# Sign of a converted weight by a VectorE mask and a GpSimd add, routing in three portions, ones by GpSimd

## The chip, the core and the metric

One core of a Trainium2 chip runs the whole program. The metric is device microseconds for one execution, as the median of several runs.

## The reference, cut to what matters

```python
def phi(x):                                   # per head, 64 -> 128 -> 256 features
    proj = x @ w_phi
    proj = proj - max(abs(proj))
    return concat([exp(proj), exp(-proj)])
kv = phi(k).T @ v;  z = sum(phi(k))           # per batch and head
attn = (phi(q) @ kv) / (phi(q) @ z + 1e-06)   # 4 x 8 x 576 x 64
x = attn as [2304, 512]
e = argmax(x @ w_gate);  gate = softmax prob of e     # 8 experts
y = gate * (relu(x @ w1[e]) @ w2[e])          # at most `capacity` tokens per expert
h = y @ w_in;  out = (h - tanh(h)) @ w_out    # 512 -> 2048 -> 512
```

`w_in` and `w_out` arrive as 64-bit floats. The kernel reads each as two 32-bit words, makes an fp32 number of it on the chip, and splits that into a high and a low part for products in three matmuls.

## The kernel before, in words

There are two stages. In the **attention stage** (about the first 183 us) a loop over steps `s` works on 18 chunks of 128 tokens. Step `i` issues to TensorE (PE), in this order: the projection of the keys of chunk `i` into the PSUM pair `xb` (L303), the transposes of an earlier query chunk (L378), the products keys times values of chunk `i-1` (L346), the projection of the queries of chunk `i-5`, again into `xb`, the numerators (L445), and a small gate product of chunk `i` (L332). Each projection is followed on VectorE (DVE) by a reduction and a subtraction out of `xb` (L311, L314), here called "k pair" and "q pair"; the next projection into `xb` waits for the subtraction. ScalarE (ACT) does the exponentials (L322, L323 for keys, L384 for queries) and the evacuations. The third engine with data work is GpSimd (POOL), and SP issues most DMAs. All engines work in program order; the order is written by hand in the loop at L747 to L842.

Woven into steps 4 to 17 is the conversion of 13 pieces of weights of 128x1024 (`pieces`, `CV`). ACT scales the high word into `a` (L91) and takes its sign into a bf16 tile `m` (L94); DVE shifts `a` left (L98, right after the k pair) and or-s in the top bits of the low word (L100, at the end of the step); GpSimd multiplies `a` by `m` (L104). In the next step ACT copies `a` into the high part (L274) and GpSimd subtracts it from `a` for the low part (L277).

Routing (`route1`) is a chain of small DVE instructions on three chunks at once. For groups of chunks 0 to 2, 3 to 5 and 6 to 8 it runs after the q pair and before L100: five portions of the generator (6 instructions, L486 to L496) in the first step after the group's numerators are out, the other 8 in the next step.

A values tile `v` has three buffers. Its DMA (L241) also writes over a column of ones and the gate columns, and ACT fills both after it landed: the gate columns by L336, the ones by L337, at the end of step `i`. Two chunks (4 and 13) straddle two batches; each uses two of the tiles, whose other half DVE sets to zero (L240). So the tiles of chunks 5, 6, 14 and 15, and the second ones of 4 and 13, are loaded one step later than the others.

In the **expert stage** the experts and the two last weight products run over units of 576 slots; here six more rows of `w_out` are converted (`late_bits`, L1112), four with GpSimd's multiply and two with DVE's.

Of the kernel before, what the change touches and what calls it, by code (L numbers as in the profile page):

```python
# [37 lines left out]
def build(nc, tc, ctx, qT, kT, vT, v, w_phi, w_gate, w12, win, wout, out, cap):  # L38
# [46 lines left out]


    NP = 512

    def cv_size(t, a):

        nc.scalar.activation(out=a.bitcast(F32), in_=t[:, :, 1].bitcast(F32), func=AF.Copy, scale=2.0 ** -112)  # L91

    def cv_sign(t, m):
        nc.scalar.activation(out=m, in_=t[:, :, 1].bitcast(F32), func=AF.Sign)  # L94

    def cv_bits(t, a, m, eng=nc.gpsimd):

        nc.vector.tensor_scalar(out=a, in0=a, scalar1=3, scalar2=None, op0=ALU.logical_shift_left)  # L98
        yield
        nc.vector.scalar_tensor_tensor(out=a, in0=t[:, :, 0], scalar=29, in1=a,  # L100
                                       op0=ALU.logical_shift_right, op1=ALU.bitwise_or)
        yield
        af = a.bitcast(F32)
        eng.tensor_tensor(out=af, in0=af, in1=m, op=ALU.mult)  # L104
        yield

    def cv_split(af, fh, fl, eng=nc.gpsimd):
# [29 lines left out]
    def attention():  # L137
# [97 lines left out]
        def ldv(c, a):  # L235
            t = vuse[c][a]
            lo, hi = (64 * a, 64 * a + 64) if c in strad else (0, P)
            if c in strad:
                z = 64 - 64 * a
                nc.vector.memset(t[z:z + 64, :, 0:HB], 0.0)  # L240
            nc.sync.dma_start(out=t[lo:hi].rearrange("p h d -> p (h d)"), in_=v[c, lo:hi])  # L241

        def ldq(c):
# [18 lines left out]
        def cv_mag(i):  # L262
            if i in raw:
                a = cva[i] = cv.tile([P, NPC], I32, tag="a", name="a")
                m = cvm[i] = cv.tile([P, NPC], BF16, tag="m", name="m")
                cvw[i] = a.bitcast(F32)
                cv_size(raw[i], a)
                cv_sign(raw[i], m)

        def cv_main(i):  # L270
            yield from cv_bits(raw.pop(i), cva.pop(i), cvm.pop(i))
# [27 lines left out]
        def proj(kind, i, ps):  # L299
            src = (kin if kind == "k" else qin)[i]  # L300
            for hp in range(4):
                for g in range(2):
                    nc.tensor.matmul(ps[:, g, hp * DF:(hp + 1) * DF],  # L303
                                     src[64 * g:64 * g + 64, hp * P:(hp + 1) * P], wphi[64 * g:64 * g + 64],
                                     start=(hp == 0), stop=(hp == 3), skip_group_check=True)
            psk[kind, i] = ps.rearrange("p g (a b) -> p (g a) b", b=DF)
# [12 lines left out]
        def kexp(i):  # L319
# [3 lines left out]
            nc.scalar.activation(out=e[:, :, 1, :], in_=t, func=AF.Exp, scale=-1.0)  # L323
            kp[i] = e

        def vgate(c):
            vg = sb[:, 0:4 * GP].rearrange("p (a b) -> p a b", b=GP)
            ps = vg[:, :, 0:2 * E].rearrange("p a (b e) -> p a b e", e=E)
            for hp in range(4):
                for a in range(2):  # L330
                    o = hp * P + 64 * a
                    nc.tensor.matmul(vg[64 * a:64 * a + 64, hp, :], vtin[c][:, o:o + 64], wgb[:, hp],  # L332
                                     start=(hp == 0), stop=(hp == 3), skip_group_check=True)
            for a, t in enumerate(vuse[c]):
                lo, hi = (64 * a, 64 * a + 64) if c in strad else (0, P)
                nc.scalar.copy(t[lo:hi, :, D + 1:HB].rearrange("p (a b) e -> p a b e", b=2), ps[lo:hi])  # L336
                nc.scalar.copy(t[lo:hi, :, D:D + 1], ones[lo:hi, 0:H].unsqueeze(2))  # L337

        def kv(i, vt, first, last):
            for g in range(2):  # L340
# [406 lines left out]
        for s in range(LAST + 1):  # L747
            i, j, jt = s, s - LAG, s - LAG - 1
            jn = jt if s < SD else jt - 1 if s > SD else -1
            kk, qq, tt = i < NCH, 0 <= j < NCH, 0 <= jt < NCH  # L750
            pc, pd = CV.get(s), CV.get(s - 1)
            since = {cs: s - (cs[-1] + LAG + 1) for cs in subs}
            if s == SK:
                stk.close()
                mo["alloc"]()
                qpools.append(stq.enter_context(tc.tile_pool(name="qp2", bufs=1)))
                mo["spare"](qpools[-1])
                mo["rows"](zero)
            if kk:
                proj("k", i, xb if i > LAG or i % 2 == 0 else yb)  # L760
            if tt:
                trans(jt)
                qexp(jt, 0)
                qexp(jt, 1)
            if since[subs[-1]] == 3:
                prefix(early)
            if 0 <= i - 1 < NCH - 1:
                kv_step(i - 1)
            if kk:
                for _ in sub("k", i):  # L770
                    pass
            bits = iter(()) if pc is None else cv_main(pc)
            next(bits, None)
            if qq:
                proj("q", j, xb)
            if i - 1 in strad:
                kv_second(i - 1)
            if i == NCH:
                kv_step(i - 1)
                first_ids()  # L780
            if pd is not None:
                cv_hi(pd)
                cv_lo(pd)
            if kk:
                kexp(i)
            wgen = iter(())
            if since[subs[-1]] == 3:
                wgen = itertools.chain(route2(early), table(early))
                run(itertools.islice(wgen, 5))
            if qq:  # L790
                for _ in sub("q", j):
                    pass
            smalls = []
            for cs in subs:
                d = since[cs]
                if d == 1:
                    rgen[cs] = route1(early, cs[0], cs[-1] + 1)
                    smalls.append(itertools.islice(rgen[cs], 5))
                if d == 2:
                    smalls.append(rgen[cs])  # L800
            smalls.append(wgen)
            if s == NCH:
                smalls.append(fgen["t"])
            if s == SK:
                smalls.append(fgen["u"])
            weave([], smalls)
            flush()
            for _ in bits:
                pass
            if 0 <= jn < NCH:  # L810
                num(jn)
            if kk:
                vgate(i)
            if CV.get(s + 1) is not None:
                cv_mag(CV[s + 1])
            if s + 2 < NCH:
                ldk(s + 2)
            if 0 <= j + 2 < NCH:
                ldq(j + 2)
            if pc is not None:  # L820
                cv_load(pc + NRAW)
            if s == SK:
                mo["first"]()
            if s + 2 < NCH:
                ldvt(s + 2)
            for c, a in vslot.get(s, []):
                if c > 1:
                    ldv(c, a)
            if s in (2, 3):
                cv_load(s - 2)  # L830
            if 0 <= jn < NCH:
                xstore([jn])
            for c in zeros.get(s, ()):
                nc.sync.dma_start(out=out[c * P:(c + 1) * P, :].rearrange("t (a b) -> t a b", a=4),
                                  in_=zero.unsqueeze(1).to_broadcast([P, 4, P]))
            if s >= SK:
                mo["drain"](s - SK)
            if s == SK + 3:
                rgen["a"] = route1(tailg, 0, NA)
                run(itertools.islice(rgen["a"], 5))  # L840
            if s == SK + 4:
                run(rgen["a"])  # L842
# [9 lines left out]
    def experts():  # L852
# [252 lines left out]

        def late_tiles(f):
            if f in lord[LF:]:
                return rawt[0][:, 0:NP].bitcast(I32), rawt[1].bitcast(BF16)[:, 0:NP]
            a = (hs, y1)[f % 2].rearrange("p a b -> p (a b)")[:, 0:NP].bitcast(I32)
            return a, ut[:, f % 2].bitcast(BF16)[:, 0:NP]  # L1110

        def late_bits(f, eng=nc.gpsimd):  # L1112
            a, m = late_tiles(f)
            for t, lo, hi in late_parts(f):
                cv_size(t, a[:, lo:hi])
                cv_sign(t, m[:, lo:hi])
            for t, lo, hi in late_parts(f):
                yield from cv_bits(t, a[:, lo:hi], m[:, lo:hi], eng)

        def late_split(f, eng=nc.gpsimd):  # L1120
            cv_split(late_tiles(f)[0].bitcast(F32), *wo[f], eng)
# [33 lines left out]
        def unit(j, prev):  # L1155
# [57 lines left out]
            for s, (b, p) in enumerate(seq2):  # L1213
# [17 lines left out]
                if j == 0:  # L1231

                    for k, f in enumerate(lord[LF:]):
                        if s == 3 * k - 1:
                            late_load(f)
                        elif s == 3 * k + 1:
                            lbits[f] = late_bits(f, nc.vector)
                            next(lbits[f])
                        elif s == 3 * k + 2:
                            for _ in lbits[f]:  # L1240
                                pass
                        elif s == 3 * k + 3:
                            late_split(f, nc.vector)
# [150 lines left out]
```

## Time and profile before

| | us |
|---|---|
| median of 3 runs (lowest, highest) | 683.21 (681.22, 683.97) |
| the profiled execution's own time | 679.38 |
| its span in the trace | 677.3 |

The profile is of one execution; its own time is 2.08 us above its span, and lies 3.83 us under the median of the runs. Durations and waits are read from the span; a time for the changed kernel is a difference set against the median. Times in the trace count from the span's start.

### The profile page before, as it was taken

To read this page: it belongs to the slowest core of one execution; us is meant where nothing else is said; L and a number is where in the kernel's file an instruction comes from. 1 tells how busy PE (TensorE), PEld (TensorE's weight loads), DVE (VectorE), ACT (ScalarE), POOL (GpSimd) and SP (SyncE) were. 2 spreads that over 40 slices of the span, in tenths; PEclk is the share of its full clock that TensorE was granted. 3 is DMA by queue.
4 is the path that set the end of the run, shared out by engine and by line. 5 is a ranking of instruction groups with operands and counts; after the bars stand their busy time and mean duration, and the time that the engine had idled before them with its cause. 6 is when DMAs were issued, how large, how long until landed. Compare 5 with 4: busy or idle time off the path is not lost. (4 is left out here: it accounts for less than half of the span.)

```text
span 677.3 us, 17365 instructions
## 1 busy us (share of the span) xinstructions
PE 640.7 (95%) x7107; PEld 623.9 (92%) x7107; DVE 516.0 (76%) x758; ACT 427.4 (63%) x741; POOL 240.5 (36%) x184
## 2 busy tenths in 40 slices
PE   8799898999999999999999999999999999999993
PEld 6788887888899989999999999999999999999992
DVE  3797888887877678889876638888976547888982
ACT  3698988877744677677544536668645527658661
POOL 1155454455200445433640104633460102553361
PEclk7999999999999999999999999999999999999997
DMA  5878686879465602002224600101214530100221
GB/s 169 299 269 286 247 288 196 295 217 307 138 184 176 198 16 59 25 32 74 70 66 158 185 23 32 37 1 39 82 46 153 166 107 1 40 13 1 86 70 40
DMA packets 46442, 82.87 MB, mean 122 GB/s; under 512 B 7392, under 2 KB 16736, under 8 KB 44688
## 3 DMA queue, kind: packets, MB, share of 16 engines
q1 hardware_dynamic: 43024, 73.44, 33.3%
q0 software_dynamic: 2624, 8.13, 4.2%
q8 instruction: 58, 0.95, 0.6%
q14 instruction: 32, 0.26, 0.1%
q10 hardware_dynamic: 704, 0.08, 0.1%
HBM read 68.59 MB, written 13.05 MB: 121 GB/s over the span
## 5 line engine op out<-in xcount | busy, mean ns | idle before, releaser
L1005 POOL TENSOR_SCALAR al<-ut 128x576 fp32r<-128x576 f32 (+1 forms) x51 | 84.5, 1657 | 151.4 <-ACT ut L1001 82.7
L900 DVE TENSOR_TENSOR w<-raw,w 128x512 fp32r<-128x512 f32 x102 | 71.0, 712 | 46.4 <-ACT w L895 42.8
L895 ACT CAST w<-raw 128x512 fp32r<-128x512 f32 x102 | 61.8, 619 | 60.2 <-DMA raw<-w 31.5
L913 PE MATMUL xb<-xh,w_in_h 128*128 128x288 f32 x264 | 79.6, 301 | 1.1 <-ACT ut L1001 1.1
L915 PE MATMUL xb<-xh,w_in_l 128*128 128x288 f32 x264 | 78.5, 297 | 0.0
L914 PE MATMUL xb<-xl,w_in_h 128*128 128x288 f32 x264 | 78.3, 296 | 0.0
L1052 POOL DMA_INDIRECT out<-row,ids x18 | 20.5, 1137 | 116.0 <-DVE row L1050 75.0
L992 DVE TENSOR_TENSOR al<-y,ah 128x576 fp32r<-128x576 f32 (+1 forms) x51 | 40.6, 796 | 24.3 <-ACT ah L991 24.3
L1000 ACT COPY hs<-xb 128x576 f32<-128x576 f32 (+1 forms) x36 | 21.5, 598 | 58.3 <-DVE th L1023 29.8
L311 DVE TENSOR_REDUCE m<-xb 128x8 f32<-128x1024 f32 x33 | 40.3, 1220 | 23.3 <-PE xb L303 23.2
L914 PE MATMUL kvb<-al,w_oa_h 128*128 128x288 f32 x180 | 53.5, 297 | 0.8 <-DVE al L992 0.8
L913 PE MATMUL kvb<-ah,w_oa_h 128*128 128x288 f32 x180 | 53.3, 296 | 0.3 <-ACT ah L991 0.3
L915 PE MATMUL kvb<-ah,w_oa_l 128*128 128x288 f32 x180 | 53.3, 296 | 0.0
L1016 DVE SCALAR_TENSOR_TENSOR y<-y,ut 128x576 f32<-128x576 f32 (+1 forms) x51 | 41.3, 809 | 14.5 <-ACT y L1004 14.5
L346 PE MATMUL kvb<-v,kp 128*64 128x74 f32 x1280 | 47.4, 234 | 4.7 <-ACT v L337 4.0
L346 PEld LDWEIGHTS kvb<-v,kp 128*64 128x64 f32 x1280 | 44.3, 141 | 8.1 <-ACT v L337 5.2
L913 PEld LDWEIGHTS xb<-xh,w_in_h 128*128 128x128 f32 x264 | 49.8, 189 | 1.3 <-ACT ut L1001 1.3
L1019 DVE SCALAR_TENSOR_TENSOR y<-y,y 128x576 f32<-128x576 f32 (+1 forms) x51 | 44.8, 879 | 7.4 <-ACT y L1006 5.9
L914 PEld LDWEIGHTS xb<-xl,w_in_h 128*128 128x128 f32 x264 | 49.8, 189 | 0.0
L915 PEld LDWEIGHTS xb<-xh,w_in_l 128*128 128x128 f32 x264 | 49.6, 188 | 0.0
L104 POOL TENSOR_TENSOR a<-a,m 128x1024 f32<-128x1024 f32 x13 | 27.8, 2140 | 54.9 <-DVE a L100 54.9
L1024 DVE COPY_PREDICATED y<-al,th 128x576 f32<-128x576 int32 (+1 forms) x51 | 42.7, 838 | 5.6 <-DVE th L1023 0.5
(291 smaller groups left out, 2159.9 us busy)
## 6 DMA issues: line engine op xcount, KB each, us to landing
raw<-w SPq DMA_DIRECT2D x105, 256.0 KB, 3.0
raw<-win SPq DMA_DIRECT2D x8, 1024.0 KB, 5.1
raw<-wout SPq DMA_DIRECT2D x5, 1024.0 KB, 5.4
v<-v SPq DMA_DIRECT2D x16, 296.0 KB, 5.9
k<-kT SPq DMA_DIRECT2D x18, 256.0 KB, 6.0
vt<-vT SPq DMA_DIRECT2D x18, 256.0 KB, 5.4
q<-qT SPq DMA_DIRECT2D x18, 256.0 KB, 5.7
xs<-x SPq DMA_DIRECT2D x18, 256.0 KB, 6.3
```

Of the source, the lines that this page charges most:

```text
L311: nc.vector.tensor_reduce(out=m, in_=ps, axis=AX.X, op=ALU.max, apply_absolute_value=True)
L346: nc.tensor.matmul(kvb[bank][64 * a:64 * a + 64, col * NKV:col * NKV + VS], kp[i][:, 4 * g + hp, s, 64 * a:64 * a + 64], vt[:, 2 * hp + g, :],
L895: nc.scalar.copy(d[:, 0], t)
L900: eng.tensor_tensor(out=d[:, 1], in0=t, in1=d[:, 0].bitcast(F32), op=ALU.subtract)
L913: nc.tensor.matmul(o, ah, bh, start=first, stop=False, skip_group_check=True)
L914: nc.tensor.matmul(o, ah, bl, start=False, stop=False, skip_group_check=True)
L915: nc.tensor.matmul(o, al, bh, start=False, stop=last, skip_group_check=True)
L992: nc.vector.tensor_tensor(out=AL[a][:, i], in0=y2[:, i], in1=AH[a][:, i].bitcast(F32), op=ALU.subtract)
L1005: nc.gpsimd.tensor_scalar(out=AL[a][:, i], in0=ut[:, i], scalar1=C2, scalar2=None, op0=ALU.is_gt)
L1016: nc.vector.scalar_tensor_tensor(out=y1[:, i], in0=y1[:, i], scalar=T1, in1=ut[:, i], op0=ALU.add, op1=ALU.mult)
L1019: nc.vector.scalar_tensor_tensor(out=y2[:, i], in0=y2[:, i], scalar=T2, in1=y1[:, i], op0=ALU.add, op1=ALU.mult)
L1024: nc.vector.copy_predicated(y2[:, i], AL[a][:, i].bitcast(I32), th[:, i])
```

## The change

The sign is no longer a factor. DVE masks the high word with the sign bit into a whole-number tile `m` (now 32-bit, one buffer instead of two), ahead of the left shift; GpSimd adds `m` to `a` as a whole number. ACT's sign instruction is gone everywhere, and in the expert stage all six conversions use GpSimd's add. `route1` of the first two groups runs in three steps (2, 3 and the remaining portions), of the third group in two as before. GpSimd writes the ones (`vones`, emitted at the start of step `i`) and zeroes the halves of the straddling tiles; ACT's copy and DVE's memset are gone.

```diff
-    def cv_sign(t, m):
-        nc.scalar.activation(out=m, in_=t[:, :, 1].bitcast(F32), func=AF.Sign)
-
-    def cv_bits(t, a, m, eng=nc.gpsimd):
+    def cv_bits(t, a, m):
+        nc.vector.tensor_scalar(out=m, in0=t[:, :, 1], scalar1=SIGN, scalar2=None, op0=ALU.bitwise_and)
+        yield
         nc.vector.tensor_scalar(out=a, in0=a, scalar1=3, scalar2=None, op0=ALU.logical_shift_left)
         yield
         nc.vector.scalar_tensor_tensor(out=a, in0=t[:, :, 0], scalar=29, in1=a,
                                        op0=ALU.logical_shift_right, op1=ALU.bitwise_or)
         yield
-        af = a.bitcast(F32)
-        eng.tensor_tensor(out=af, in0=af, in1=m, op=ALU.mult)
+        nc.gpsimd.tensor_tensor(out=a, in0=a, in1=m, op=ALU.add)
         yield
...
-                nc.vector.memset(t[z:z + 64, :, 0:HB], 0.0)
+                nc.gpsimd.memset(t[z:z + 64, :, 0:HB], 0.0)
...
-                m = cvm[i] = cv.tile([P, NPC], BF16, tag="m", name="m")
+                m = cvm[i] = cv.tile([P, NPC], I32, tag="m", name="m", bufs=1)
                 cvw[i] = a.bitcast(F32)
                 cv_size(raw[i], a)
-                cv_sign(raw[i], m)
...
+        def vones(c):
+            for a, t in enumerate(vuse[c]):
+                lo, hi = (64 * a, 64 * a + 64) if c in strad else (0, P)
+                nc.gpsimd.memset(t[lo:hi, :, D:D + 1], 1.0)
...
-                nc.scalar.copy(t[lo:hi, :, D:D + 1], ones[lo:hi, 0:H].unsqueeze(2))
...
             if kk:
+                vones(i)
                 proj("k", i, xb if i > LAG or i % 2 == 0 else yb)
...
-            next(bits, None)
+            run(itertools.islice(bits, 2))
...
-                    smalls.append(itertools.islice(rgen[cs], 5))
-                if d == 2:
-                    smalls.append(rgen[cs])
+                if 1 <= d <= 3 and cs in rgen:
+                    cut = (5,) if cs == subs[-1] else (2, 5)
+                    smalls.append(itertools.islice(rgen[cs], *cut[d - 1:d]) if d <= len(cut) else rgen[cs])
...
-                cv_sign(t, m[:, lo:hi])
             for t, lo, hi in late_parts(f):
-                yield from cv_bits(t, a[:, lo:hi], m[:, lo:hi], eng)
+                yield from cv_bits(t, a[:, lo:hi], m[:, lo:hi])
...
-                            lbits[f] = late_bits(f, nc.vector)
+                            lbits[f] = late_bits(f)
```

## Rows read from the trace of the kernel before

**Rows 1.** The page: busy time, share of the span and instructions of each engine.
```profile
PE 640.7 (95%) x7107; PEld 623.9 (92%) x7107; DVE 516.0 (76%) x758; ACT 427.4 (63%) x741; POOL 240.5 (36%) x184
```
**Rows 2.** PE's waits, 0 to 183 us, then 183 to 300: us, times, longest.
```profile
PE xb L303 <- DVE d L314: 6.6, 6, 2.2
PE kvb L346 <- ACT v L337: 4.0, 5, 1.3
...
PE xb L913 <- ACT ut L1001: 1.1, 1, 1.1
```
**Rows 3.** Windows, one per step (7, 10 to 13): length, then each engine's busy time.
```profile
47.38:55.46 8.08, 8.08 (x188) 7.56 (x184) 7.00 (x7) 7.78 (x13) 4.99 (x3) 1.00 0.86 296
73.59:83.73 10.14, 8.14 (x188) 7.56 (x184) 9.16 (x13) 8.54 (x15) 5.50 (x3) 1.00 0.55 190
83.73:92.47 8.74, 8.15 (x188) 7.56 (x184) 7.80 (x15) 7.86 (x12) 4.51 (x2) 1.00 0.70 217
92.47:101.41 8.94, 8.22 (x188) 7.56 (x185) 7.93 (x8) 7.41 (x10) 3.86 (x2) 1.00 0.98 345
101.41:111.79 10.38, 8.15 (x188) 7.56 (x185) 9.34 (x14) 8.26 (x15) 5.28 (x3) 1.00 0.63 206
```
**Rows 4.** Groups of instructions by shape: busy us, mean ns, idle before.
```profile
L337 ACT CAST v<-ones 128x8 f32<-128x8 bf16 x16 | 3.6, 225 | 0.0
...
L314 DVE TENSOR_TENSOR d<-xb,m 128x1024 f32<-128x1024 f32 x33 | 40.4, 1225 | 1.9
...
L100 DVE SCALAR_TENSOR_TENSOR a<-raw,a 128x1024 int32<-128x1024 int32 x13 | 19.7, 1513 | 0.0
...
L98 DVE TENSOR_SCALAR a<-a 128x1024 int32<-128x1024 int32 x13 | 8.9, 685 | 1.3 <-ACT a L91 1.2
...
L240 DVE MEMSET v<- 64x584 f32 x4 | 2.2, 545 | 1.7 <-PE kvb L346 1.4 <-issue 0.2
...
L513 DVE TENSOR_TENSOR r<-r,mx 128x24 f32<-128x24 f32 x3 | 0.5, 183 | 0.1
...
L104 POOL TENSOR_TENSOR a<-a,m 128x1024 f32<-128x1024 f32 x13 | 27.8, 2140 | 54.9 <-DVE a L100 54.9
...
L277 POOL TENSOR_TENSOR w_in_l<-a,w_in_h 128x1024 fp32r<-128x1024 f32 x8 | 19.0, 2380 | 22.3 <-ACT w_in_h L274 22.3
```
**Rows 5.** Timeline from the end of step 9 into step 10: start, duration.
```profile
72.20 2.38 POOL L277 TENSOR_TENSOR w_in_l<-a,w_in_h 128x1024 fp32r<-128x1024 f32 x1 [4.00 <-ACT w_in_h L274]
...
73.44 1.18 DVE L486 TENSOR_SCALAR r<-dl 128x24 f32<-128x24 f32 x1
...
74.99 0.36 DVE L489 TENSOR_TENSOR lgx<-dl,r 128x192 f32<-128x192 f32 x1
...
76.24 1.22 DVE L100 SCALAR_TENSOR_TENSOR a<-raw,a 128x1024 int32<-128x1024 int32 x1
...
77.54 2.13 POOL L104 TENSOR_TENSOR a<-a,m 128x1024 f32<-128x1024 f32 x1 [2.96 <-DVE a L100]
...
79.84 0.68 DVE L98 TENSOR_SCALAR a<-a 128x1024 int32<-128x1024 int32 x1
...
81.19 1.23 DVE L311 TENSOR_REDUCE m<-xb 128x8 f32<-128x1024 f32 x1 [0.66 <-PE xb L303]
```
**Rows 6.** Timeline of ACT in step 4.
```profile
28.56 1.17 ACT L94 ACTIVATE m<-raw 128x1024 bf16<-128x1024 f32 x1
...
29.61 1.05 ACT L322 ACTIVATE kp<-d 128x1024 f32<-128x1024 f32 x1
```
**Rows 7.** Timeline of step 6, then L241's DMAs: us from issue to landing.
```profile
42.02 1.14 SPq L241 DMA_DIRECT2D v<-v  x2
...
45.45 2.38 POOL L277 TENSOR_TENSOR w_in_l<-a,w_in_h 128x1024 fp32r<-128x1024 f32 x1 [2.12 <-ACT w_in_h L274]
...
47.23 1.68 DVE L100 SCALAR_TENSOR_TENSOR a<-raw,a 128x1024 int32<-128x1024 int32 x1
...
DMA to landing us min/median/max: 3.0/5.9/8.4
```

More of the change, by code (lines that the diff above doesn't have):

```diff
@@ L87, in build @@
     NP = 512
+    SIGN = -(1 << 31)
     def cv_size(t, a):
         nc.scalar.activation(out=a.bitcast(F32), in_=t[:, :, 1].bitcast(F32), func=AF.Copy, scale=2.0 ** -112)
-    def cv_sign(t, m):
-        nc.scalar.activation(out=m, in_=t[:, :, 1].bitcast(F32), func=AF.Sign)
-    def cv_bits(t, a, m, eng=nc.gpsimd):
+    def cv_bits(t, a, m):
+        nc.vector.tensor_scalar(out=m, in0=t[:, :, 1], scalar1=SIGN, scalar2=None, op0=ALU.bitwise_and)
+        yield
         nc.vector.tensor_scalar(out=a, in0=a, scalar1=3, scalar2=None, op0=ALU.logical_shift_left)
@@ L1107, in late_tiles, with late_bits @@
             if f in lord[LF:]:
[L1108 to L1112, printed above, removed]
+                return rawt[0][:, 0:NP].bitcast(I32), rawt[1][:, 0:NP].bitcast(I32)
+            return [x.rearrange("p a b -> p (a b)")[:, 0:NP].bitcast(I32) for x in ((hs, y1)[f % 2], ut)]
+        def late_bits(f):
             a, m = late_tiles(f)
```

## The prediction

> **What bounds the kernel now.** I read the page first. PE is busy 95% of the span and no other engine over 76% [rows 1], so an edit to ACT, DVE and GpSimd can only win where PE stands still. PE's waits come next [rows 2]: from 183 to 300 us, where the expert stage begins and the late conversions lie, the longest is 1.1 us, so there is next to nothing to give. Before it, the two largest entries are 6.6 us in six waits for the subtraction out of `xb` (L314, DVE), and 4.0 us in five waits for the ones column (L337, ACT). The trace therefore has to be read in the attention stage, step by step. The windows show that [rows 3]: step 7 takes 8.08 us and PE is busy for all of it, with ACT at 7.78 and DVE at 7.00. That is the floor. Steps 10 and 13 take 10.14 and 10.38 with PE at 8.15, and there DVE is the longest at 9.16 and 9.34: these are the steps behind the first routing portion of a group. So three engines lie within about a microsecond of each other, and what is taken from one may land on the next.
>
> Why step 10 is long is seen in the timeline [rows 5]. The first routing portion fills DVE from 73.44 until L100 starts at 76.24, 2.80 us. Its first instruction handles 24 elements and takes 1.18 us: it ends at 74.62, 0.04 after GpSimd's L277 does (72.20 + 2.38). L100 in step 6 does the same [rows 7]: begun at 47.23 it takes 1.68, ending 1.08 after L277 (45.45 + 2.38 = 47.83), where it takes 1.22 alone [rows 5]. So while GpSimd runs a two-input instruction, some DVE instructions on SBUF operands stand. After L100 come the k pair and L98, and the q pair starts only at 81.19, 0.66 of it spent waiting for PE's q projection, which could itself not start before the k pair was done.
>
> **The change part by part.** *Sign off ACT.* 13 of L94 at 1.17 us [rows 6] and the ones copies at 0.22 [rows 4] leave ACT: in step 7, 7.78 becomes some 6.5. PE gains only where it waited for ACT. In the first steps the ones copy is the last link before the kv product; copies issue so densely that only about 0.1 us of each is on the path (an estimate: half of its 0.22). In step 4 the key exponential starts at 29.61 behind L94 at 28.56 [rows 6] and would move up by as much as their distance of 1.05, less by what it then waits for. Bounds 0.3 and 1.5; I take **-0.55**, near the lower end because the next step must still wait for a piece of weights to land.
>
> *Mask on DVE.* 13 masks of 128x1024 whole numbers, out of every second word. The nearest row by kind is L98, the same operation class at 0.685; the nearest by source is L100, which reads the other word at the same stride and takes 1.22 alone. I take 0.68, since L98's half duration goes with one source and L100 has two; the price of the upper end is below. The mask lies between the k pair and L98, while PE does the q projection. L98 ended at 80.52 and the q pair started at 81.19 when PE's projection was there: 0.66 us of cover [rows 5]. In PE-bound steps the mask is thus hidden; without the cover it costs 0.65 a step. DVE's 7.00 of step 7 becomes 7.7, still under 8.08.
>
> On this duration the Trainium skill has two rules. Its page "Vector Engine (DVE) Microarchitecture Reference", section 5.1 ("Performance modes — why throughput varies by op and dtype"), gives two elements a cycle to one source and a destination in SBUF with an even outer dimension, and asks for no unit step: by it the mask is an L98, and the sum stays as it is. Its section 5.2 ("Measured stream behaviour on trn2") speaks against the change: a port keeps its full rate only over runs of two adjacent words, and this source has runs of one; its line for one such source, 1.73 against 1.05 ns a column, would make an estimated 1.1 us of the mask's 0.68, which is close to rival B. L100 with this stride is not slower than L314 with dense operands (1.22 against 1.225), so the trace does not bear out the second.
>
> *Add on GpSimd.* 13 adds take the place of L104 (2.14). Both inputs are now 4 bytes wide, like those of L277 (2.38). No row shows a whole-number add: bounds 2.0 and 3.0, I take 2.38. Nothing waited for L104 in DVE before; now the next mask does, because `m` has one buffer. The cover is L100's end to the next mask: in step 10, L100 ends at 77.46 and L98 starts at 79.84, 2.38 later; the old multiply ended at 79.67. At 2.38 plus the start lag of 0.08 the mask waits about 0.1 in such a step and nothing in PE-bound ones; it holds up L98, then the q pair, then PE's next projection.
>
> *Routing in three portions, memset off DVE.* First portion after: L486 to L489, done at 75.35 instead of 76.24, so L100 is 0.89 earlier in step 10; second portion 0.89 (75.35 to 76.24) instead of the old second's 1.46 (eight instructions like L513, 0.183 [rows 4]); those 1.46 come a step later, where there were none. What each step costs now is a DVE sum: portion + L100 1.22 + k pair 2.45 + mask and L98 1.4 (with the 0.1 above) + q pair 2.45.
> Step 10: 1.9 + 7.5 = 9.4 against 10.14: -0.74.
> Step 11: 0.9 + 7.5 = 8.4, with handover to and from PE 8.6, against 8.74: -0.14.
> Step 12: 1.5 + 7.5 = 9.0 against 8.94: +0.06. Here DVE also loses the 0.55 memset [rows 4], which the 7.5 does not hold.
> Step 13: first portion 1.4 (L277 starts up to one L94 earlier, so the stand is shorter) + 7.5 = 8.9 against 10.38: -1.48.
> Step 14, with the same second portion as step 11 but a second kv product on PE: -0.35.
> Together **-2.65**. The third group is cut as before and its masks lie under PE work: 0.
>
> *Ones on GpSimd.* 20 small memsets, and 4 that took DVE 0.55 us [rows 4], on an engine that is 36% busy [rows 1] are nothing in themselves. But `vones(i)` now stands ahead of L277 and of the add in GpSimd's queue, and it waits for the values DMA. For most chunks that DMA was issued in the step before last and has landed. For the late ones it has not: in step 6 the DMAs are issued at 42.02, land 5.9 later by the median, at 47.9, and L277 had started at 45.45 [rows 7]. L277 goes to some 47.5, where it meets L100 (47.23). Whoever is first, the other stands: L277 ends at 49.9 to 51, the add 2.4 later at 52 to 53, and the mask of step 7, due at about 51.5, is 0.6 to 2 late, and with it the q pair and PE. With a 3.0 us landing the cost is 0, with 8.4 it is 3. I take **+1.3**. Steps 5, 13, 14 and 15 have the same late tiles; there L277 ends clear of L100, or L100 comes before it and no longer stands, so 0, with up to +1.2 each as the bad end.
>
> *Late conversions.* Six masks of half the size and two adds moved to GpSimd, in the stage where PE waits for 1.1 us at most: 0.
>
> Sum: -0.55 - 2.65 + 1.3 = **-1.9 us**. Against the profiled execution 679.38 this is 677.5. That execution lies 3.83 under the median; set against the median, 683.21 - 1.9 = **681.3 us**, 0.3% less.
>
> **The rivals.** (A) *The stands go too.* If the values land early in step 6 (+1.3 falls away) and L277, an L94 slot earlier, clears L486 in steps 9 and 15 (1.0 each), the sum is -1.9 - 1.3 - 2.0 = -5.2: **678.0**. For it: ACT's 1.05 ahead of L277. Against: ACT's copy waits for GpSimd's add as well, and that gets longer.
> (B) *The mask is slow.* At 1.22 it adds 0.54 to about five DVE-bound steps and some 0.1 to the eight others: +3.5, a sum of +1.6: **684.8**. For it: L100's stride and 1.22. Against: L98.
> (C) *The add is slow*, the rival on the slower side. A mask in a PE-bound step may start until about 2.7 us after L100's end (k pair 2.45, then the cover left by the mask). Every 0.1 us beyond 2.7 costs 0.1 in each of 12 steps. From 2.86 the change loses, from 3.15 it loses over 0.5%; at 3.5 it is 12 x 0.8 - 1.9 = +7.7: **690.9**. For it: no row has such an add. Against: L104 and L277, 2.14 and 2.38.
> (D) *The sign work was hidden anyway*, and the routing stalls return as DVE's own load: -0.55, -2.65 and +1.3 shrink to about 0: **683.2**.
>
> **How the numbers follow.** About 0.5%, 3.4 us, is what a measurement of this kernel can tell from no change. Forecast 0.34, A 0.30, B 0.12, C 0.12, D 0.12. Faster by over 0.5%: A, and 0.04 of the forecast, 0.34. Slower: C, 0.04 of B and 0.03 of a forecast whose late tiles cost their bad ends: 0.19. The rest, 0.47, is the same. The range runs from A less 0.8, 677.2, to the point where C passes 0.5%, 686.6; it leaves about 0.08 below and 0.1 above.
>
> **What would show it.** The mask at 0.68, the add at 2.1 to 2.5, the two waits of 2 us before the q projection of steps 10 and 13 cut to about 1 or less; DVE the longest engine in steps 10 to 13; GpSimd's ones in step 6 waiting for the values DMA, and behind them L277 touching L100. The forecast is wrong if the mask's or the add's duration misses, if PE's waits move to the mask's wait for `m`, or if the stage's end near 183 us does not move while the routing waits are gone.

## The result and the profile after

The changed kernel took 688.52 us by the median of four runs (687.98 to 689.62), against 683.38 for the kernel before beside it: a ratio of 1.0083, with an interval of 1.0057 to 1.0109. It is slower by 0.8%; the forecast was 681.3, and the predicted range ended at 686.6. A later comparison of the same two kernels, with 12 runs of the changed one, gave 683.87 us and 1.0038 [1.0011, 1.0066]; the kernel before against itself gave 1.0020 [0.9987, 1.0053]. So by the medians the loss is 0.4 to 0.8%, and each ratio is good to about 0.3%.

The page's line of the engines, after:
```profile
PE 647.2 (94%) x7107; PEld 629.0 (92%) x7107; DVE 524.5 (76%) x773; ACT 409.3 (60%) x700; POOL 250.4 (36%) x210
```
ACT lost 18 us of work and DVE and POOL gained 8.5 and 9.9 [rows 1], as the change says. The groups by shape (busy us, mean ns of one, idle before and its releaser):
```profile
L96 DVE TENSOR_SCALAR m<-raw 128x1024 int32<-128x1024 int32 x13 | 9.8, 758 | 4.4 <-POOL a L103 4.3
...
L103 POOL TENSOR_TENSOR a<-a,m 128x1024 int32<-128x1024 int32 x13 | 30.8, 2371 | 18.6 <-DVE a L100 18.6
...
L327 POOL MEMSET v<- 128x8 f32 x16 | 2.3, 141 | 30.5 <-DMA v<-v 30.4
L327 POOL MEMSET v<- 64x8 f32 x4 | 0.4, 107 | 11.0 <-DMA v<-v 11.0
```
The two disputed prices are as forecast: the add takes 2.37, and the mask 0.69 where nothing stands in its way (rows of step 14 and 16 below; the mean holds some stands). The mask reads every second word and costs what the dense L98 does [rows 4], so the rule for runs of adjacent words (the Trainium skill, "Vector Engine (DVE) Microarchitecture Reference", section 5.2) is not borne out for this instruction. What the groups show beside it is 41 us in which GpSimd's queue stood at the ones memset, waiting for the values DMA. It stood another 11.8 at the memsets that zero the straddling tiles, which wait for TensorE; that part of the change stays in every variant of the changed kernel and was not tried alone.

TensorE's waits, 0 to 183 us, then 183 to 310 us (us in total, times, longest), answer to [rows 2]:
```profile
PE kvb L348 <- issue: 6.0, 6, 1.8
PE xb L301 <- DVE d L312: 5.7, 10, 1.9
PE xb L301 <- issue: 1.9, 5, 0.5
PE yb L447 <- ACT qp L386: 1.8, 1, 1.8
PE kvb L348 <- ACT v L339: 1.7, 1, 1.7
...
PE xb L916 <- ACT ut L1004: 2.9, 1, 2.9
PE kvb L918 <- DVE w L903: 1.7, 2, 1.4
```
The largest entry lies in the first steps. The key-value product still waits there, 0.73 us in three like steps that had 0.79; the profile names no releaser ("issue") where it had named the ones copy. The wait for the subtraction is nearly as large as before, but in ten places of which the longest is in another step. And the second stretch, which had 1.1 us at most, now has 2.9 and 1.4. The windows of steps 7, 10 to 14 and 16 (columns as in [rows 3]) say where:
```profile
49.46:58.22 8.76, 8.15 (x185) 7.57 (x185) 8.60 (x8) 6.76 (x10) 6.23 (x4) 1.00 0.59 198
74.38:83.19 8.81, 8.15 (x189) 7.56 (x185) 8.59 (x11) 6.74 (x10) 5.46 (x4) 1.00 0.71 231
83.19:91.85 8.66, 8.15 (x189) 7.56 (x185) 8.29 (x13) 7.17 (x12) 4.85 (x3) 1.00 0.86 308
91.85:100.63 8.78, 8.26 (x189) 7.60 (x185) 8.48 (x14) 7.17 (x11) 6.28 (x4) 1.00 0.76 233
100.63:109.14 8.51, 8.22 (x184) 7.56 (x185) 8.28 (x11) 6.06 (x7) 2.94 (x3) 1.00 0.93 304
109.14:121.86 12.72, 10.27 (x248) 9.61 (x248) 12.34 (x18) 8.67 (x16) 6.26 (x5) 1.00 0.56 191
130.32:142.42 12.10, 8.29 (x189) 7.59 (x185) 8.75 (x14) 6.69 (x11) 6.89 (x5) 1.00 0.72 251
```
Steps 14 and 16 of the kernel before:
```profile
111.79:122.58 10.79, 10.21 (x253) 9.62 (x249) 9.85 (x15) 9.63 (x17) 4.54 (x2) 1.00 0.75 247
132.64:140.72 8.08, 8.08 (x187) 7.56 (x185) 7.09 (x10) 7.51 (x12) 4.52 (x2) 1.00 0.66 207
```
Steps 10 to 13 are 34.76 us long where they were 38.20, a gain of 3.4 (forecast 2.3). Steps 14 and 16 give it back: they were 10.79 and 8.08. (Step 15 went from 10.06 to 8.46; the three together from 28.93 to 33.28.) Step 7 is longer too, 8.76 in place of 8.08 [rows 3]: the ones of chunk 6 hold the subtraction until 48.48, and L100 then stands as the prediction had it:
```profile
49.32 2.61 DVE L100 SCALAR_TENSOR_TENSOR a<-raw,a 128x1024 int32<-128x1024 int32 x1
```
Rows picked from the timelines of step 14 (start, duration; in brackets idle before and releaser):
```profile
109.89 0.11 POOL L327 MEMSET v<- 64x8 f32 x1 [4.34 <-DMA v<-v]
110.07 2.38 POOL L275 TENSOR_TENSOR w_oa_l<-a,w_oa_h 128x1024 fp32r<-128x1024 f32 x1
110.14 3.38 DVE L100 SCALAR_TENSOR_TENSOR a<-raw,a 128x1024 int32<-128x1024 int32 x1
112.48 1.21 ACT L92 ACTIVATE a<-raw 128x1024 f32<-128x1024 f32 x1 [1.37 <-POOL w_oa_l L275]
115.99 0.69 DVE L96 TENSOR_SCALAR m<-raw 128x1024 int32<-128x1024 int32 x1
116.05 1.16 PE L301 MATMUL xb<-wphi,q 64*128 64x128 f32 x16 [1.93 <-DVE d L312]
```
The memset, for the second tile of chunk 13, belongs to step 13 of the loop; its wait ends when TensorE is already in step 14. It heads the queue and waits 4.34 us; the subtraction behind it therefore starts 0.07 before L100, which stands until it is done (3.38 in place of 1.22 [rows 5]); the k pair is late and TensorE's projection waits 1.93. In step 16 the delay, now at the tile of chunk 15, goes another way:
```profile
133.85 0.22 ACT L339 COPY v<-sb 128x64 f32<-128x64 f32 x1 [3.13 <-DMA v<-v]
133.88 0.12 POOL L327 MEMSET v<- 128x8 f32 x1 [7.38 <-DMA v<-v]
133.94 2.37 POOL L275 TENSOR_TENSOR w_oa_l<-a,w_oa_h 128x1024 fp32r<-128x1024 f32 x1
134.17 2.27 PE L348 MATMUL kvb<-v,kp 128*64 128x74 f32 x64 [1.66 <-ACT v L339]
136.28 2.36 POOL L103 TENSOR_TENSOR a<-a,m 128x1024 int32<-128x1024 int32 x1
136.35 1.16 ACT L92 ACTIVATE a<-raw 128x1024 f32<-128x1024 f32 x1 [2.28 <-POOL w_oa_l L275]
138.68 0.69 DVE L96 TENSOR_SCALAR m<-raw 128x1024 int32<-128x1024 int32 x1 [3.04 <-POOL a L103]
139.38 2.31 PE L447 MATMUL yb<-kvs,qp 128*64 128x74 f32 x64 [1.84 <-ACT qp L386]
```
ACT's next size instruction needs the two-buffer tile `a` back from the late subtraction; the query exponential stands behind it in ACT's order, and TensorE waits 1.84 for `qp`. At the same time the mask waits 3.04 for the late add. Neither wait names the ones, which stand ahead of both. Not all of step 16 is theirs: ACT's copy of the gate columns waited 3.13 for the same DMA, and TensorE 1.66 behind it. In the two profiles of the kernel before that copy has no such wait; without the memset at the head it still has some (2.5 in ones_act, 2.6 in route_only below).

In the expert stage the last two late conversions stand out, on VectorE and GpSimd:
```profile
286.46 1.74 POOL L103 TENSOR_TENSOR raw<-raw,raw 128x512 int32<-128x512 int32 x1 [4.73 <-DVE raw L100]
286.97 1.85 DVE L1019 SCALAR_TENSOR_TENSOR y<-y,ut 128x576 f32<-128x576 f32 x1
289.77 2.58 DVE L1024 SCALAR_TENSOR_TENSOR y<-y,hs 128x576 f32<-128x576 f32 x1
290.04 1.06 POOL L935 TENSOR_TENSOR row<-row 96x512 f32<-96x512 f32 x1
291.05 1.68 POOL L1008 TENSOR_SCALAR al<-ut 128x576 fp32r<-128x576 f32 x1
292.27 2.09 DVE L1026 TENSOR_TENSOR th<-hs,th 128x576 f32<-128x576 f32 x1
292.68 1.06 POOL L935 TENSOR_TENSOR row<-row 96x512 f32<-96x512 f32 x1
```
The add, on GpSimd in place of VectorE's multiplication, pushes GpSimd's row work (L935) and its L1008 back, into the VectorE steps of a gate (the elementwise work between two products of the stage); three of these take 1.85, 2.58 and 2.09 where an undisturbed one takes 0.75.

### The profile page after: what moved, and what is told of

The parts are those of the page before. It is cut to its first block, busy times and chain, and to the rows that moved or that the text cites. A ratio compares the mean times of both kernels' runs of the same rounds, so it can differ in the third digit from the quotient of the medians.

```text
span 686.5 us, 17396 instructions
## 1 busy us (share of the span) xinstructions
PE 647.2 (94%) x7107; PEld 629.0 (92%) x7107; DVE 524.5 (76%) x773; ACT 409.3 (60%) x700; POOL 250.4 (36%) x210
## 4 chain that ended last, share of the span: by engine, by line
PE 51%; DVE 19%; DMA 12%; ACT 8%; issue 4%; POOL 4%; SPq 0%; ACTq 0%; DVEq 0%; POOLq 0%
DMA out<-row,ids 6%; PE kvb L918 5%; PE kvb L916 5%; PE kvb L917 5%; PE xb L916 3%; PE yb L916 3%; PE xb L917 3%; PE xb L918 3%; PE yb L918 3%; PE yb L917 3%; PE xb L301 3%; DMA raw<-w 2%; DVE y L1024 2%; DMA v<-v 2%; DVE y L1022 2%
## 5 line engine op out<-in xcount | busy, mean ns | idle before, releaser
L1008 POOL TENSOR_SCALAR al<-ut 128x576 fp32r<-128x576 f32 (+1 forms) x51 | 83.7, 1641 | 144.9 <-ACT ut L1004 69.9
L918 PE MATMUL xb<-xh,w_in_l 128*128 128x288 f32 x264 | 79.1, 299 | 0.0
L918 PE MATMUL kvb<-ah,w_oa_l 128*128 128x288 f32 x180 | 53.3, 296 | 0.0
L918 PEld LDWEIGHTS xb<-xh,w_in_l 128*128 128x128 f32 x264 | 50.3, 190 | 0.0
L1009 ACT ACTIVATE y<-ut,sq_b 128x576 f32<-128x576 f32 (+1 forms) x51 | 38.1, 748 | 12.4 <-DVE al L995 11.4
```

Source lines behind the costliest of these rows:

```text
L918: nc.tensor.matmul(o, al, bh, start=False, stop=last, skip_group_check=True)
L1008: nc.gpsimd.tensor_scalar(out=AL[a][:, i], in0=ut[:, i], scalar1=C2, scalar2=None, op0=ALU.is_gt)
```

## The experiments

Two lengths are read from each profile beside the time: from the k projection's start in step 5 to that in step 17 ("attention"), and from ScalarE's first read of a gate pair to its sixteenth ("gates"). The expectations in us were set against the first comparison; beside the runs below the kernel before took 679.8 to 681.5, so that a time alone stands some 2 to 4 us lower, and the ratios decide.

| kernel | median us | ratio to before, 95% | attention us | gates us |
|---|---|---|---|---|
| before, again | 680.71 | 1.0020 [0.9987, 1.0053] | 113.55 (first profile 111.33) | 95.80 (first profile 95.83) |
| changed | 688.52 | 1.0083 [1.0057, 1.0109] | 111.90 | 99.42 |
| changed, again | 683.87 | 1.0038 [1.0011, 1.0066] | 112.65 | 99.12 |
| ones_act | 680.23 | 1.0006 [0.9972, 1.0039] | 107.73 | 99.33 |
| late_old | 679.78 | 0.9995 [0.9959, 1.0030] | 112.88 | 96.40 |
| ones_late_old | 675.97 | 0.9929 [0.9899, 0.9959] | 105.97 | 95.86 |
| route_only | 678.40 | 0.9995 [0.9963, 1.0026] | 109.34 | 95.90 |
| mask_only | 678.09 | 0.9946 [0.9913, 0.9979] | 108.58 | 96.34 |
| first4_old | 679.52 | 0.9979 [0.9944, 1.0015] | 106.76 | 99.41 |
| last2_old | 678.17 | 0.9949 [0.9916, 0.9982] | 111.50 | 96.31 |
| ones_later | 705.59 | 1.0353 [1.0297, 1.0409] | 128.08 | 100.48 |
| ones_between | 680.38 | 0.9984 [0.9951, 1.0018] | 105.70 | 99.17 |
| between_late_old | 674.53 | 0.9918 [0.9890, 0.9947] | 108.01 | 96.32 |
| or_late | 676.33 | 0.9930 [0.9904, 0.9957] | 106.29 | 95.84 |
| or_all | 684.22 | 1.0040 [1.0003, 1.0078] | 114.59 | 95.81 |

**ones_act.** The ones written by ACT again:
```diff
+                nc.scalar.copy(t[lo:hi, :, D:D + 1], ones[lo:hi, 0:H].unsqueeze(2))
...
-                vones(i)
```


> The changed kernel with one part undone: the ones column is written by ScalarE's copy behind the gate columns, as before, and GpSimd's queue has no memset that waits for the late values DMA. Theory 1 (the queued memset is the main loss of the attention stage: steps 6, 8, 14 and 16 end 2 to 4 us later than they would): the k projection of step 17 moves from +1.7 us to about -2.5 us against the kernel before, and the whole time falls by 3 to 5 us, to 683.5 to 685.5. Theory 2 (nearly all the loss is in the late conversions of the expert stage): the time falls by 0 to 1.5 us, to 687 or more. Theory 3 (the wait of VectorE's mask on the single-buffered m tile behind GpSimd's add is the attention stage's loss): steps 14 and 16 stay as long as they are, 12.7 and 12.1 us, and the time stays within 1 us of 688.5.

The k projection of step 17 came 3.0 us before that of the kernel before (137.72), where the changed kernel's came 1.7 after it. Theory 1 stands for this stage; by the ratios alone, 1.0006 against 1.0038, it is within the uncertainty. Step 16 fell to 9.21 us, step 14 only to 12.29, with 1.4 of "issue" in its numerators. Theory 3, the mask's one-buffer tile, falls: that tile is unchanged here, and the mask's waits for the add, 4.3 us in the changed kernel, are gone.

**late_old.** The six late conversions as before, in the changed kernel:
```diff
-                yield from cv_bits(t, a[:, lo:hi], m[:, lo:hi])
+                yield from old_bits(t, a[:, lo:hi], m[:, lo:hi], eng)
```
(with the sign by ACT behind the size, and `m` in its old places).


> The changed kernel with the six late conversions of the expert stage done as before: sign by ScalarE, multiplied in, the last two on VectorE, and the m half of the tile ut. Attention stage as changed. Theory 2 (late conversions cost about 5 us around the first gate and the last two of them): the first gate comes about 1 to 2 us sooner and the stretch from there to 310 us is 3.5 to 5 us shorter; time 683.5 to 685. If the late conversions cost nothing, as I predicted, time stays at 688 to 689 and the loss of the expert stage is fetch or clock.

The gates fall from 99.1 to 99.4 us to 96.40, within 0.6 of before: theory 2 is right for the gates, and my zero was wrong. By the ratios (0.9995 against 1.0038) that is 0.4%. Steps 14 and 16 stay long (14.50 and 9.68), as theory 1 has it.

**ones_late_old.** Both edits above.


> Both parts undone: ones by ScalarE, and late conversions as before; what is left of the change is the mask and add in the attention stage, the memset of the straddling values on GpSimd and the routing in three portions. If theories 1 and 2 hold and add up, 679.5 to 681.5 (the 2.65 us of the routing and the 0.5 us of the signs are left as a gain against 683.4). If theory 3 (mask and add in the attention stage cost too), 683 to 686.

0.9929: the forecast gain is there (3.2 us as the sum of its terms without the ones; measured 4.8, with 2.8 to 6.9 as its interval). On this chip the median is 3.8 us below late_old's, which has the ones on GpSimd, and 4.3 below that of ones_act, which has the new late conversions. Some waiting is left where the experts begin: ahead of the transposes at 167.6 us TensorE waited 3.4 for DVE (1.4 and 2.6 in the two profiles of the kernel before), in whose queue the first expert weights stood; ACT's cast of these had waited 3.5 for their DMA.

**route_only** and **mask_only.** The kernel before with one part each: the three portions, and the mask and add in the attention stage.


> The kernel before with the routing of a group in three portions and nothing else of the change. My prediction's term for it, with the memset, was -2.65 us, nearly all of it in steps 10 and 13: 680.5 to 681.0 expected, with steps 13 and 14 started 1.5 to 2 us sooner. If the stalls that it removes are put back by later steps, 683 to 684.

> The kernel before with the conversions of the attention stage alone changed: VectorE's mask of 0.69 us and GpSimd's add of whole numbers in place of ScalarE's sign and the multiplication. My prediction gave it -0.55 us for the signs off ScalarE. Between the run of the routing alone (678.4) and that of routing, mask and memset (675.97) lie 2.4 us. If that is the mask's, 678 to 679; if my small term is right and the rest is the scatter between executions, 680 to 681.

The routing shortens the attention by 2.0 us against the first profile of before, which is no more than the two profiles of before differ, and its ratio can't be told from 1 (0.3 us less, with some 2 us either way). Its steps 10 and 13 are 0.95 and 1.67 shorter, near their forecast, but 12 and 14 are 0.60 and 0.92 longer. The mask with its add is worth 0.54%, 3.7 us [1.4, 5.9], against the 0.55 us that I gave the signs. Its step 12 shows one place where:
```profile
91.14 1.17 ACT L92 ACTIVATE a<-raw 128x1024 f32<-128x1024 f32 x1 [1.21 <-DMA raw<-wout]
92.22 1.92 ACT L400 ACTIVATE qp<-yb 128x1024 f32<-128x1024 f32 x2
94.86 2.31 PE L461 MATMUL yb<-kvs,qp 128*64 128x74 f32 x64
95.15 2.39 POOL L288 TENSOR_TENSOR w_in_l<-a,w_in_h 128x1024 fp32r<-128x1024 f32 x1 [2.29 <-ACT w_in_h L285]
97.37 0.20 DVE L502 TENSOR_SCALAR r<-dl 128x24 f32<-128x24 f32 x1
```
The same step of the kernel before:
```profile
95.72 1.15 ACT L94 ACTIVATE m<-raw 128x1024 bf16<-128x1024 f32 x1
98.74 2.31 PE L445 MATMUL yb<-kvs,qp 128*64 128x74 f32 x64 [0.68 <-ACT qp L384]
100.51 1.60 DVE L486 TENSOR_SCALAR r<-dl 128x24 f32<-128x24 f32 x1
```
With the mask the query exponential follows the size directly, and TensorE doesn't wait for `qp` (0.68 before). GpSimd's subtraction is earlier with it and all but done when the routing's first instruction comes, which takes 0.20 where it took 1.60.

**ones_later** and **ones_between.** The memset stays on GpSimd but elsewhere in its step: behind the add, or between the subtraction and the add.
```diff
 # ones_later
             for _ in bits:
                 pass
+            if kk:
+                vones(i)
 # ones_between
                 cv_lo(pd)
+            if kk:
+                vones(i)
```


> The changed kernel, late conversions and all, with one edit: the memset of the ones stays on GpSimd but is issued late in its step, behind the conversion's add, instead of first in the step ahead of the subtraction. Theory 1 (it is the place in GpSimd's in-order queue, ahead of the subtraction, while the values DMA is still under way): the subtraction starts with its step again, and the time is that of the kernel with ones by ScalarE, 679.5 to 681.5. Rival (GpSimd's write of the ones itself costs, wherever it stands, because the key-value product waits for it): 683 to 688.

> The changed kernel with the memset of the ones on GpSimd between the subtraction and the add of its step. In first place it holds the subtraction back (the changed kernel), in last place the key-value product waited 21.1 us for it in eleven steps (705.6 us). Theory 1 in its mended form (GpSimd's own order decides: behind the subtraction the values DMA has mostly landed, and ahead of the add nothing is waiting for it): TensorE's waits for the memset vanish, the subtraction starts with its step, and the time is that of ones by ScalarE, 679.5 to 681.5. Rival (any wait for the values DMA in GpSimd's queue costs, since the add then comes late and the mask and the cast behind it): 683 to 687.

The first expectation failed outright: 705.6 us. TensorE's waits for the memset in it, and then in ones_between:
```profile
PE kvb L348 <- POOL v L327: 21.1, 11, 3.4
```
```profile
PE kvb L348 <- POOL v L327: 1.2, 1, 1.2
```
Behind the add the memset comes after the moment at which the key-value product wants it. Between the two it costs neither: 0.9984 and an attention of 105.70, the shortest of all. So it is the place in GpSimd's order, not the engine; the mended theory 1 holds. On the same chip the changed kernel took 683.87, 3.5 us more, with intervals that overlap by less than 0.1%.

**first4_old** and **last2_old.** On the base of ones_act, the first four or the last two late conversions as before.


> Ones by ScalarE, and the first four late conversions as before (sign by ScalarE, multiplied in by GpSimd, m in its own half of ut); the last two with mask and add. The kernel with ones by ScalarE alone took 680.23 us, with all six as before 675.97. Theory 2a (the loss is in the last two: their add stands on GpSimd where it was VectorE's, 1.73 us, and pushes GpSimd's weighing and GELU steps into the gate's VectorE steps, which then take 1.85, 2.58 and 2.09 us in place of 0.76): nearly nothing comes back, 679 to 681, and those three rows stay. Theory 2b (the loss is in the first four, around the first gate, where the mask waits 0.73 us for the add on the shared m): 676 to 677.5, and the first gate's weight split is no longer late (1.4 us of TensorE's wait).

> Ones by ScalarE, and the last two late conversions as before (sign by ScalarE, multiplied in by VectorE); the first four with mask and add on GpSimd. Theory 2a: 676 to 678, the gate's three VectorE steps back at 0.76 us each, and TensorE's wait of 2.9 us for ScalarE's read at about 288 us falls to about 1.1. Theory 2b: 679 to 681.

By the gates it is clear: 99.41 with the last two new, 96.31 with them old. That is theory 2a, 3.1 us; the times, 1.35 us apart on one chip, don't separate the two. All six profiles with the last two new have 99.1 to 100.5, the ten others 95.8 to 96.4. The five VectorE steps of the gate above sum to 8.14 us, in last2_old to 4.67. Part of the loss is clock. Windows of 4 us of the changed kernel and of last2_old (TensorE busy second, its granted clock third from the end):
```profile
292.00:296.00 4.00, 1.13 (x10) 0.94 (x8) 3.74 (x4) 1.55 (x3) 2.01 (x3) 0.98 0.00 0
296.00:300.00 4.00, 4.00 (x21) 4.00 (x21) 3.55 (x5) 2.59 (x5) 2.58 (x2) 0.59 0.40 131
```
```profile
288.00:292.00 4.00, 2.91 (x24) 2.72 (x23) 3.50 (x6) 2.52 (x5) 1.41 (x1) 1.00 0.04 14
292.00:296.00 4.00, 4.00 (x32) 4.00 (x31) 3.69 (x5) 2.01 (x4) 1.44 (x2) 1.00 0.37 121
```
After standing 2.9 us TensorE got a mean of 0.59 of its clock for 4 us, mostly its lower level (1.2 of 2.4 GHz), and did 21 matmuls where it else did 32; after standing 1.1 it kept 1.00. In all six profiles with the last two new TensorE stood 2.8 to 2.9 us at this place and its clock then fell; in the ten others it stood 1.1 to 1.2, and it didn't. The longer stand is 1.8 us, and the 11 matmuls are another 1.4 (an estimate, at the 4 us for 32 of the last line): together 3.2, about the 3.1 of the gates. The first four give back 0.27% by the ratios (1.0006 to 0.9979), which is within their uncertainty; their 1.4 us of TensorE's wait for the split weight (L918 in the changed kernel) stands in last2_old too and is gone in ones_late_old. last2_old's attention of 111.50 is out of line with the six others that have no memset at the queue's head (105.70 to 108.01): TensorE's longest waits there are 2.7 for ACT's gate columns, whose copy had waited 2.7 for the values DMA, and 2.6 of "issue". So the late values DMA can hold ACT's copies too.

**after_again** and **before_again.** Nothing edited.


> The changed kernel once more, with nothing edited, for a second profile and for a time on the same chip as its variants. If the 4.3 us that TensorE lost between 164 and 168.7 us in the first profile (single matmuls with 0.3 to 0.5 us of issue between them) are of the change, they stand in this profile too; if they belong to that execution alone, the projection there takes 1.2 us, and the time is 686 to 689 with a scatter of some 3 us either way.

> The kernel before against itself on the same chip, with a second profile. If the first comparison (1.0083) and the second (1.0038) of the changed kernel differ by the scatter between executions, this ratio lies within 0.4% of 1, and its own times spread over some 8 us; its k projections of steps 5 and 17 stand 111 us apart, as in the first profile, if that stretch is steady from one execution to another.

In the first profile of the changed kernel TensorE lost 4.2 us in one query projection, with matmuls one at a time; the second has none of it (first lines: changed; then changed again):
```profile
164.37 0.27 PE L301 MATMUL xb<-wphi,q 64*128 64x128 f32 x1 [0.30 <-issue]
165.09 0.36 PE L301 MATMUL xb<-wphi,q 64*128 64x128 f32 x1 [0.46 <-issue]
```
```profile
166.82 1.16 PE L301 MATMUL xb<-wphi,q 64*128 64x128 f32 x16
```
So it belongs to that execution and not to the change. The time, 683.87, is below the 686 to 689 that I expected; whether the other runs of the first comparison had such a loss, no trace shows. The kernel before spreads from 677.26 to 685.88 against itself, and its attention stretch by 2.2 us, more than I expected.

**between_late_old, or_late, or_all.** The first mends both places and keeps the rest of the change. The others start from ones_late_old and put the sign in with one VectorE instruction, in the last two late conversions or in those and the attention stage:
```diff
+        nc.vector.scalar_tensor_tensor(out=a, in0=t[:, :, 1], scalar=SIGN, in1=a, op0=ALU.bitwise_and, op1=ALU.bitwise_or)
```


> The changed kernel with the ones memset between GpSimd's subtraction and add, and all six late conversions as before. If these two places are the whole loss, this is the kernel of ones by ScalarE with late conversions as before (676.0, ratio 0.993), less ScalarE's 0.2 us per step of ones: 674.5 to 676.5, ratio 0.990 to 0.994. If a part of the loss lies elsewhere in the change, 677.5 or more.

> The kernel of ones by ScalarE and late conversions as before, with the last two late conversions done otherwise: VectorE puts the sign bit in with one instruction (and with the sign mask, or into the word) of about 0.69 us, in place of ScalarE's sign and VectorE's multiplication of 1.04 us; nothing on GpSimd. 675 to 676.5 expected: at most 0.35 us of VectorE and 0.66 us of ScalarE in two gate steps, beside 675.97.

> As the kernel before this one, and the conversions of the attention stage too: VectorE's and-or of 1.22 us in place of its mask of 0.69 us and of GpSimd's add of 2.37 us. GpSimd's time per step falls by half, and VectorE's rises by 0.53 us a step over 13 steps. If the chain that ends a step runs over GpSimd's add (the cast waited 0.9 to 1.2 us for it at 103 and 107 us), 672 to 675; if VectorE's queue is what TensorE waits for (its waits for d), 677 to 681.

between_late_old is the best kernel of the study: 674.53 us, 0.9918 [0.9890, 0.9947], faster than before by 0.8%. or_late is no better than ones_late_old. or_all loses 1.1% to or_late: TensorE's wait for DVE's subtraction rises from 2.0 us in five places to 9.1 in ten, and the time is worse than either theory had it. So taking GpSimd's add away gave nothing there, and VectorE has no room for 0.53 us a step.

## Why the prediction was wrong

**The steps that failed.** Of the ones the prediction said that they meet L100 in step 6 (+1.3) and that in steps 5, 13, 14 and 15 "L277 ends clear of L100 [...] so 0". In step 6 the mechanism came as described, at 0.7 us in step 7. (Its working put the subtraction at 47.5, before the landing of 47.9 that it waits for; it began at 48.48.) The zeros were the error. Behind the memset of step 13 the subtraction ran exactly into L100, and step 14 became 1.9 us longer. Behind that of step 15 its lateness went through `a` to ACT, which I had not followed: I named the mask behind the add, but not the tile that ACT's next size needs back, with the query exponential queued behind it. Step 16 became 4.0 longer, part of it by ACT's own wait for the late DMA. With the memset at the queue's head the attention took 111.9 to 112.9 us in three profiles, without it in the changed kernel's other variants 105.7 to 108.0 in six and 111.5 in one. (ones_later, and or_all, which loads VectorE more, are left out here.) In the time it is worth 0.32 to 0.54% (1.0038 against ones_act and ones_between) with the new late conversions and 0.66 to 0.77% with the old (0.9995 against 0.9929 and 0.9918), 2.2 to 5.2 us, each difference good to some 0.45%; the two pairs measured on one chip give 3.5 and 3.8 by their medians. The forecast was 1.3.

**Late conversions: 0** was the other. The argument was that TensorE waits for 1.1 us at most in that stage. But the two adds moved to GpSimd pushed its other work into VectorE's steps, as the rows of the gate show: TensorE stood 2.9 us in place of 1.1 and then ran at the lower clock, which cost 3.1 to 3.5 us in the gates alone.

**Sign off ACT** (-0.55) was right in kind and too small: with the mask -3.7 [1.4 to 5.9 less]. It was costed at the key exponential of one step, whereas the sign also stood ahead of the query exponential and the cast, and so set when GpSimd's subtraction met VectorE. The 0.1 us for each of the first ones copies was too much: 0.06 of wait went. **Routing** (-2.65): steps 10 and 13 of the changed kernel shrank by 1.33 and 1.87 (forecast 0.74 and 1.48), though part of that is the sign's; alone it gave 0.95 and 1.67 there, lost 1.5 again in steps 12 and 14, and shortened the time by nothing that could be measured.

**Right:** the mask's 0.69, the add's 2.37 (rivals B and C are out, at their own prices), DVE the longest engine in steps 10 to 13, and the two waits of 2.0 and 2.2 us ahead of the q projections of steps 10 and 13, now 0.7 and under 0.3.

The account closes by ratios. What is left when both places are mended is -0.7 to -0.8%, 4.8 to 5.6 us, in place of the forecast 3.2; ones and late conversions together cost 1.1 to 1.2% (0.9929 and 0.9918 to 1.0038), 7.4 to 8.2 us, in place of 1.3. Not settled: where the 0.4% between the two comparisons of the changed kernel comes from (the slow projection of its first profile would be as much, if its other runs had it), why the values DMA of chunk 15 lands late for ACT too, and which of the three consequences of the late subtraction (the stand of L100, ACT's wait for `a`, the mask's wait for the add) costs most; more buffers of `a` or `m` were not tried.

## What to carry to other kernels

A small instruction that waits for a DMA, put at the head of an in-order queue, costs the wait of everything behind it, and the profile blames the last of these, not the first. Before moving one, list what stands behind it and which buffers those give back, and look for the slot where its data has landed and nothing urgent follows. That the critical engine hardly waits in a stage doesn't say that work can be moved between the others there for nothing: follow whom the moved work pushes back.

## What was not expected of the hardware

- A stop of TensorE of 2.9 us was followed by 4 us at a mean granted clock of 0.59; after one of 1.1 us the clock stayed at 1.00.
- VectorE steps of 0.75 us took 1.85 to 2.58 beside GpSimd's add (1.74), row work (1.06) and L1008 (1.68).
- The kernel before, unchanged, had two profiled executions whose attention stretch differed by 2.2 us.
